# GELU MLP forward and backward on one core: the first block of x in two transposes from two queues, and a second copy moved ahead of a tanh

## The chip, the core and the metric

The kernel runs on one core of a Trainium2 chip. The metric is device time in microseconds, the median of several executions. One execution per kernel is also recorded by the hardware profiler; its trace gives the start and length of each instruction on TensorE (PE for matmuls, PEld for weight loads), VectorE (DVE), ScalarE (ACT) and GpSimd (POOL), and of each DMA issue on the queues of SyncE (SP), ScalarE and GpSimd. Times within the trace are us from the start of the profiled span.

## The reference

An MLP of one layer with the tanh form of GELU, forward and all gradients, in bf16. x is 2048 x 448, w1 448 x 1792, w2 1792 x 448.

```python
def _fwd_reference(x, w1, b1, w2, b2):
    h = jnp.einsum("bsd,df->bsf", x, w1) + b1
    h = _gelu(h)
    return jnp.einsum("bsf,fd->bsd", h, w2) + b2
...
    _out, _vjp = jax.vjp(_f, x, w1, b1, w2, b2)
    _grads = _vjp(grad_out)
    return (_out0, *[jnp.asarray(_g) for _g in _grads])
```

The outputs are the forward result, and the gradients of x, w1, b1, w2 and b2.

## The kernel before

**Tiling.** The 2048 rows are cut into four blocks of 512 (SB), taken in the order 512, 1024, 1536, 0 (ROW0). The 1792 hidden columns are 14 tiles of 128, taken as seven pairs per block in the order FP = 1, 2, ..., 6, 0. A step is one pair of one block, 28 steps in all. The 448 model columns are three full tiles of 128 and a tail of 64.

**A step.** For a pair, PE makes u = x w1 transposed (hidden columns on the partitions, 512 rows along the free dimension): six matmuls of 512 columns over the full tiles (`pe_u_fulls`, L207) and, for each half of the pair, a tail matmul of 64 partitions (`u_tail`, L222), which needs the tail rows of w1 (`wt1`) and closes the accumulation. `copy_u` brings u with its bias to SBUF: on ACT (L262) or DVE (L264). ACT makes its square (L271), its gelu (hT, L268) and, once DVE has made the cubic Z from the square (`dve_cubic`, L275 and L276), a tanh of it (`act_tanh`, L280). DVE turns these into the factor of the derivative (`dve_gate`, L284 to L291). PE makes q, the gradient with respect to h, from grad_out and w2 transposed (`q_tail` L229, `pe_q_fulls` L253), and DVE multiplies both into ghT (`dve_gh`, L294). The matmuls of the output and of the gradient of x follow in pieces (L323).

**Phases.** After the steps come the gradients of w1 (L562, L573) and w2 (L594) with x, grad_out, h and the h gradient in natural layout, while DVE sums the bias gradients.

**Order.** The kernel is written under a manual schedule: every engine runs its instructions in the order in which they are written, and the framework puts the waits between the engines. Queue order is also the order written. No wait is written out by hand.

**The start.** `zero` is cleared by DVE (L134). x's first block is brought in transposed, as xT (128 partitions, 4 column tiles, 512 rows), by one DMA transpose issued on SP's queue (`load_x`, L103). ScalarE's queue loads w1's columns 256 to 512 in two DMAs, the full tiles (L120) and the tail rows (L121); then it runs a gelu on one column, which brings in the activation table (L142), and loads the columns 512 to 768 in two further DMAs. SP's queue goes on with w1's columns 768 to 1024, two tiles of w2, the first block of grad_out transposed (`load_g`, gT, L113), the first part of w2 transposed (`load_w2T`, w2T, L128) and the rest in turn. All transposes of the kernel stand on SP's queue. PE runs 15 matmuls on `zero` (L168), nine of 512 columns and six of 256, before the first u.

After that PE makes u of step 0, and the order of the first steps is written out: copy of u(0) on ACT and DVE, square, gelu, cubic, u(1), tanh(0), the copies of u(1) on ACT, its square and gelu, u(2) and so on; from step 1 on a loop has a fixed order.

Of the kernel before, what the change touches and what calls it, by code (L numbers as in the profile page):

```python
# [11 lines left out]
BF16 = mybir.dt.bfloat16  # L12
# [7 lines left out]
def kernel(  # L20
# [15 lines left out]
    nc = tc.nc  # L36
    P = 128
    B, S, D = x.shape
# [4 lines left out]
    KF = D // P  # L43
    DL = D - KF * P
    SB = 512
# [3 lines left out]
    NSTEP = NB * NPAIR  # L49
    NSINGLE = 8  # L50
    LEAD = 2
    STG = 5
    ROW0 = [SB, 2 * SB, 3 * SB, 0]
    WIDE = (0, 1)
# [3 lines left out]
    x2 = x.rearrange("b s d -> (b s) d")  # L58
# [4 lines left out]
    const = ctx.enter_context(tc.tile_pool(name="const", bufs=1))  # L63
    dram = ctx.enter_context(tc.tile_pool(name="dram", bufs=1, space=bass.MemoryType.DRAM))
    psum = ctx.enter_context(tc.tile_pool(name="psum", bufs=1, space=bass.MemoryType.PSUM))
    blk = ctx.enter_context(tc.tile_pool(name="blk", bufs=2))
    tmp = ctx.enter_context(tc.tile_pool(name="tmp", bufs=2))
    stg = ctx.enter_context(tc.tile_pool(name="stg", bufs=STG))

    hT_dram = dram.tile([F, S], BF16, name="hT_dram")  # L70
    hT_dram_v = hT_dram.rearrange("(ft p) s -> p ft s", p=P)

    zero = const.tile([P, SB], BF16, name="zero")
    b1_rows = const.tile([32, P], BF16, name="b1_rows")
    b1_t16 = const.tile([P, 32], BF16, name="b1_t16")
    b1T = const.tile([P, NF], F32, name="b1T")
# [2 lines left out]
    w1_f = const.tile([P, KF, F], BF16, name="w1_f")  # L79
    w2T = const.tile([P, KF + 1, F], BF16, name="w2T")  # L80
    wt1 = const.tile([P, F], BF16, name="wt1")
# [6 lines left out]
    def one_bank(n, name):  # L88
        return psum.tile([P, SB], F32, name=name, tag=f"one{n}")

    def two_banks(n, name):
        return psum.tile([P, 2, SB], F32, name=name, tag=f"two{n}")

    xT, gT = {}, {}

    def wide(src, r0, n, shift):
        return bass.AP(src.tensor, src.offset + r0 * D - shift, [[D, n], [1, (KF + 1) * P]])

    def load_x(b):
        t = blk.tile([P, KF + 1, SB], BF16, name="xT", tag="xT")  # L100
        r0 = ROW0[b]
        if b in WIDE:
            nc.sync.dma_start_transpose(out=t[:], in_=wide(x2, r0, SB, 0))  # L103
        else:
            nc.sync.dma_start_transpose(out=t[:, 0:KF, :], in_=x2[r0:r0 + SB, 0:KF * P])
            nc.sync.dma_start_transpose(out=t[:, KF, :], in_=x2[r0:r0 + SB, D - P:D])
        xT[b] = t

    def load_g(b):
# [6 lines left out]
            nc.sync.dma_start_transpose(out=t[:, 0, :], in_=g2[r0:r0 + SB, 0:P])  # L116
        gT[b] = t

    def load_w1(eng, f0, f1):
        eng.dma_start(out=w1_f[:, :, f0:f1], in_=w1[0:KF * P, f0:f1].rearrange("(kt p) f -> p kt f", p=P))  # L120
        eng.dma_start(out=wt1[0:DL, f0:f1], in_=w1[KF * P:D, f0:f1])  # L121

    def load_w2(eng, t0, t1):
        eng.dma_start(out=w2_sb[:, t0:t1, :], in_=w2[t0 * P:t1 * P, :].rearrange("(ft p) d -> p ft d", p=P))
# [11 lines left out]
    nc.vector.memset(row0[:], 0.0)  # L136
    nc.vector.memset(row0[0:1, :], 1.0)
    nc.gpsimd.dma_start(out=b1_rows[0:NF, :], in_=b1.rearrange("(ft p) -> ft p", p=P))
    load_x(0)
    load_w1(nc.scalar, 256, 512)  # L140
    warm = stg.tile([P, 1], F32, name="warm", tag="warm", bufs=1)
    nc.scalar.activation(out=warm[:], in_=zero[:, 0:1], func=ACT.Gelu_apprx_tanh)  # L142
    load_w1(nc.scalar, 512, 768)
    load_w1(nc.sync, 768, 1024)
    load_w2(nc.sync, 2, 4)
    load_g(0)
# [17 lines left out]
    load_g(1)  # L164

    pw = two_banks(1, "pw")
    for w in [SB] * 9 + [SB // 2] * 6:
        nc.tensor.matmul(pw[:, 0, 0:w], lhsT=zero[:, 0:P], rhs=zero[:, 0:w], start=True, stop=True)  # L168
    for c in range(P // 32):
        nc.vector.transpose(b1_t16[c * 32:(c + 1) * 32, :], b1_rows[:, c * 32:(c + 1) * 32])  # L170
    nc.vector.tensor_copy(out=b1T[:], in_=b1_t16[:, 0:NF])
# [2 lines left out]
    PU, PQ = {}, {}  # L174
# [5 lines left out]
    def cols(p, a):  # L180
        return slice((2 * FP[p] + a) * P, (2 * FP[p] + a + 1) * P)

    def part(store, ks):
        return store[ks[0] // 2 % len(store)][:, 2 * (ks[0] % 2):2 * (ks[-1] % 2) + 2, :]
# [14 lines left out]
    def pe_u_fulls(f):  # L199
        b, p = divmod(f, NPAIR)  # L200
        if p == 0:
            hT[b] = blk.tile([P, NF, SB], BF16, name="hT", tag="hT")
        banks = (2, 3) if f == 1 else (0, 1) if f < NSINGLE + LEAD else order_a[2 * (f % 2):2 * (f % 2) + 2]
        PU[f] = [one_bank(n, "pu") for n in banks]
        for a in range(2):
            for kt in range(KF):
                nc.tensor.matmul(PU[f][a][:], lhsT=w1_f[:, kt, cols(p, a)], rhs=xT[b][:, kt, :], start=(kt == 0), stop=False,  # L207
                                 skip_group_check=True)

    def half(up):  # L210
        return slice(DL, P) if up else slice(0, DL)
# [1 line left out]
    def open_q(k):  # L213
        b, p = divmod(k, NPAIR)
        if p == 0:
            ghT[b] = blk.tile([P, NF, SB], BF16, name="ghT", tag="ghT")
        PQ[k] = two_banks(0 if k < NSINGLE else order_b[k % 2], "pq")

    def u_tail(f, a):
        b, p = divmod(f, NPAIR)  # L220
        hf = half(b not in WIDE)
        nc.tensor.matmul(PU[f][a][:], lhsT=wt1[hf, cols(p, a)], rhs=xT[b][hf, KF, :], start=False, stop=True,  # L222
                         tile_position=(hf.start, 0), skip_group_check=True)

    def q_tail(k, a, swap=False):
        b, p = divmod(k, NPAIR)
        hf = half((b in WIDE) != swap)
        g = g_swap[b] if swap else gT[b][:, 0, :]
        nc.tensor.matmul(PQ[k][:, a, :], lhsT=w2T[hf, 0, cols(p, a)], rhs=g[hf, :], start=True, stop=False,  # L229
                         tile_position=(hf.start, 0), skip_group_check=True)  # L230

    def pe_tails(fs, ks):
        cross = bool(fs) and bool(ks) and (fs[0] // NPAIR in WIDE) != (ks[0] // NPAIR in WIDE)
        for k in ks:
            open_q(k)
        us = [(f, a) for f in fs for a in range(2)]
        qs = [(k, a) for k in ks for a in range(2)]
        if not us and len(ks) == 2:
            for a in range(2):
                q_tail(ks[0], a)  # L240
                q_tail(ks[1], a, swap=True)
            return
        for n in range(max(len(us), len(qs))):
            if n < len(us):
                u_tail(*us[n])
            if n < len(qs):
                q_tail(*qs[n], swap=cross)
# [8 lines left out]
    def copy_u(f, engines):  # L256
        p = f % NPAIR
        for a in range(2):
            bias = b1T[:, 2 * FP[p] + a:2 * FP[p] + a + 1]
            dst = part(U4, [f])[:, a, :]  # L260
            if engines[a] == "a":
                nc.scalar.activation(out=dst, in_=PU[f][a][:], func=ACT.Identity, bias=bias)  # L262
            else:
                nc.vector.tensor_scalar(out=dst, in0=PU[f][a][:], scalar1=bias, scalar2=None, op0=ALU.add)  # L264
# [5 lines left out]
    def act_square(ks):  # L270
        nc.scalar.activation(out=part(A4, ks), in_=part(U4, ks), func=ACT.Square, scale=math.sqrt(3.0 * GELU_A * GELU_C))  # L271
# [6 lines left out]
    def act_tanh(ks):  # L278
        z = part(Z4, ks)
        nc.scalar.activation(out=z, in_=z, func=ACT.Tanh, scale=-1.0 / 3.0)  # L280
# [103 lines left out]
    def traffic(i):  # L384
# [5 lines left out]
        if i == 6:  # L390
            other_halves()

    pe_u_fulls(0)
    pe_tails([0], [])
    copy_u(0, "av")
    act_square([0])
    act_gelu([0])
    dve_cubic([0])
    pe_u_fulls(1)
    pe_tails([1], [])  # L400
    act_tanh([0])
    copy_u(1, "aa")
    act_square([1])
    act_gelu([1])
    pe_u_fulls(2)
    pe_tails([2], [])
    open_two(1, 2)
# [13 lines left out]
    for i in range(1, NSINGLE):  # L421
        f = i + LEAD
        pe_u_fulls(f)
# [219 lines left out]
```

## Time and profile before

| What | us |
|---|---|
| median of 3 runs | 273.18 (273.09 to 273.20) |
| profiled execution, device time | 273.36 |
| profiled execution, span | 271.56 |
| PE busy | 265.9 (98%) |
| DVE busy | 175.9 (65%) |
| ACT busy | 139.6 (51%) |
| warm-up matmuls L168 | 1.18 to 6.19 |
| first matmul of u(0) (L207) / first tail (L222) | 6.03 / 7.42 |
| first copy of u(0) on ACT / on DVE | 7.84 / 8.06 |

The span is the time from the first to the last instruction of the kernel in the trace; device time also has what lies around it. The chain of waits is followed back from the last instruction, at each step to what released it. Matmuls are pipelined: a row "x6, 1.46" has six matmuls whose starts lie some 0.215 apart, and the last one's latency behind them. For DMAs, an issue has a start and a length on its queue, and a time from issue to landing, after which its data may be used.

### The profile page before, as it was taken

The numbers are of one execution on the slowest core, as the hardware profiler recorded it, in microseconds if no ns is written. First come the engines' busy times: TensorE is split into PE (matmuls) and PEld (weight loads), VectorE is DVE, ScalarE is ACT, GpSimd is POOL, SyncE is SP. The second block draws the span as 40 slices with busy tenths as digits, with TensorE's granted clock in tenths as the row PEclk, the third lists the DMA queues.
The fourth block names the chain that finished last, engine by engine and source line by source line (L and its number), as shares of the span: only waits on it lengthen the run. The fifth ranks groups of instructions, "written<-read, shape, count | busy, mean of one in ns | idle before, by whom it ended". The sixth has DMA issues, their size and how long they took to land.

```text
span 271.6 us, 3646 instructions
## 1 busy us (share of the span) xinstructions
PE 265.9 (98%) x1397; PEld 127.2 (47%) x1411; DVE 175.9 (65%) x208; ACT 139.6 (51%) x163; POOL 38.4 (14%) x50
## 2 busy tenths in 40 slices
PE   8999999999999999999999999999999999999995
PEld 3334344444444545444454455554444485555554
DVE  2688999999989799685979931109999992000000
ACT  2799898799995687867668610011111121111111
POOL 1000004011001001010010102210510007900000
PEclk9999999999999999999999999999999999999999
DMA  8999799999999967074252559998111111999951
GB/s 188 224 205 238 139 213 179 167 270 249 226 265 256 239 164 170 18 191 97 93 125 75 111 108 289 377 223 199 40 41 39 39 41 30 199 212 238 196 129 34
DMA packets 112929, 44.37 MB, mean 163 GB/s; under 512 B 92000, under 2 KB 111792, under 8 KB 112912
## 3 DMA queue, kind: packets, MB, share of 16 engines
q1 hardware_dynamic: 105840, 36.20, 62.3%
q0 software_dynamic: 1824, 4.27, 5.2%
q10 hardware_dynamic: 5248, 3.67, 4.5%
q8 instruction: 11, 0.18, 0.3%
q14 instruction: 6, 0.05, 0.1%
HBM read 7.23 MB, written 14.23 MB: 79 GB/s over the span
## 4 chain that ended last, share of the span: by engine, by line
PE 87%; DVE 6%; ACT 5%; issue 1%; DVEq 0%; ACTq 0%
PE ps L323 28%; PE ps_v L594 16%; PE ps_w L562 13%; PE pq L253 11%; PE pu L207 10%; PE pu L222 4%; PE ps_w L573 2%; PE pw L168 2%; ACT A L271 1%; DVE ghT L294 1%; ACT U L262 1%; ACT hT L268 1%; DVE Z L276 1%; PE pq L229 1%; DVE Z L291 1%; DVE A L286 1%
## 5 line engine op out<-in xcount | busy, mean ns | idle before, releaser
L323 PE MATMUL ps<-w_sb,hT 128*128 128x448 bf16 x224 | 45.2, 352 | 0.2
L323 PE MATMUL ps<-w1T_sb,ghT 128*128 128x448 bf16 x224 | 43.8, 352 | 0.0
L262 ACT ACTIVATE U<-pu,b1T 128x512 bf16<-128x512 f32 x55 | 33.8, 685 | 18.3 <-PE pu L222 18.2
L594 PE MATMUL ps_v<-g_nat,h_nat 128*128 128x448 bf16 (+1 forms) x240 | 42.6, 340 | 0.0
L337 POOL DMA_DIRECT2D out_dram<-st x32 | 17.8, 558 | 162.6 <-ACT st L334 107.6
L253 PE MATMUL pq<-gT,w2T 128*128 128x512 bf16 x163 | 38.8, 380 | 0.5 <-issue 0.3
L207 PE MATMUL pu<-xT,w_f 128*128 128x512 bf16 x159 | 38.7, 379 | 0.4
L294 DVE SCALAR_TENSOR_TENSOR ghT<-Z,pq 128x1024 bf16<-128x1024 bf16 x28 | 33.8, 1220 | 7.5 <-PE pq L253 6.0
L562 PE MATMUL ps_w<-gh_nat,x_nat 128*128 128x512 bf16 (+1 forms) x192 | 36.7, 352 | 0.0
L280 ACT ACTIVATE Z<-Z 128x2048 bf16<-128x2048 bf16 (+1 forms) x18 | 27.5, 1528 | 10.4 <-DVE Z L276 10.2
L594 PEld LDWEIGHTS <-h_nat 128*128 128x128 bf16 x240 | 23.3, 98 | 19.3 <-issue 0.3
L323 PEld LDWEIGHTS <-hT 128*128 128x128 bf16 x224 | 21.8, 98 | 21.7 <-issue 1.1
L323 PEld LDWEIGHTS <-ghT 128*128 128x128 bf16 x224 | 21.9, 98 | 20.9
L548 DVE TENSOR_TENSOR acc<-acc,gh_nat 128x1792 f32<-128x1792 f32 x14 | 30.0, 2142 | 0.5
L271 ACT ACTIVATE A<-U 128x1024 bf16<-128x1024 bf16 (+1 forms) x19 | 27.7, 1456 | 0.7 <-DVE U L264 0.4
L268 ACT ACTIVATE hT<-U 128x1024 bf16<-128x1024 bf16 (+1 forms) x20 | 27.7, 1390 | 0.2
L562 PEld LDWEIGHTS <-x_nat 128*128 128x128 bf16 x192 | 18.7, 98 | 17.8 <-issue 0.4
L253 PEld LDWEIGHTS <-w2T 128*128 128x128 bf16 x168 | 15.0, 98 | 23.2 <-issue 7.6
L597 ACT CAST st<-ps_v 128x448 bf16<-128x448 f32 (+1 forms) x15 | 7.6, 507 | 34.8 <-PE ps_v L594 32.3
L207 PEld LDWEIGHTS <-w_f 128*128 128x128 bf16 x168 | 16.3, 98 | 19.1 <-issue 0.8
L334 ACT CAST st<-ps 128x448 bf16<-128x448 f32 x20 | 10.3, 529 | 27.7 <-PE ps L323 27.5
L565 ACT CAST st<-ps_w 128x512 bf16<-128x512 f32 (+1 forms) x12 | 6.4, 532 | 29.9 <-PE ps_w L562 29.9
(46 smaller groups left out, 197.3 us busy)
## 6 DMA issues: line engine op xcount, KB each, us to landing
hT_dram<-hT SPq DMA_DIRECT2D x28, 256.0 KB, 3.3
out_dram<-st POOLq DMA_DIRECT2D x32, 112.0 KB, 3.1
x_nat<-in_x_dram SPq DMA_DIRECT2D x1, 1792.0 KB, 10.2
g_nat<-in_grad_out_dram SPq DMA_DIRECT2D x1, 1792.0 KB, 16.0
out_dram<-st ACTq DMA_DIRECT2D x13, 112.0 KB, 3.3
out_dram<-st ACTq DMA_DIRECT2D x9, 128.0 KB, 1.7
w_sb<-in_w_dram SPq DMA_DIRECT2D x5, 224.0 KB, 3.9
w_f<-in_w_dram SPq DMA_DIRECT2D x5, 192.0 KB, 4.9
```

The source lines that it names most:

```text
L207: nc.tensor.matmul(PU[f][a][:], lhsT=w1_f[:, kt, cols(p, a)], rhs=xT[b][:, kt, :], start=(kt == 0), stop=False, skip_group_check=True)
L253: nc.tensor.matmul(PQ[k][:, a, :], lhsT=w2T[:, kt, cols(p, a)], rhs=gT[b][:, kt, :], start=False, stop=(kt == KF), skip_group_check=True)
L262: nc.scalar.activation(out=dst, in_=PU[f][a][:], func=ACT.Identity, bias=bias)
L268: nc.scalar.activation(out=rows(hT, r), in_=part(U4, r), func=ACT.Gelu_apprx_tanh)
L271: nc.scalar.activation(out=part(A4, ks), in_=part(U4, ks), func=ACT.Square, scale=math.sqrt(3.0 * GELU_A * GELU_C))
L280: nc.scalar.activation(out=z, in_=z, func=ACT.Tanh, scale=-1.0 / 3.0)
L294: nc.vector.scalar_tensor_tensor(out=rows(ghT, [k]), in0=part(Z4, [k]), scalar=1.0, in1=PQ[k][:], op0=ALU.add, op1=ALU.mult)
L323: nc.tensor.matmul(self.ps, lhsT=src[self.b][:, 2 * p + a, self.j * P:(self.j + 1) * P], rhs=w[:, 2 * FP[p] + a, :], start=(p == 0 and a = ...
L337: nc.gpsimd.dma_start(out=(out2 if self.kind == "o" else gx2)[r:r + P, :], in_=st[:, 0:D])
L548: nc.vector.tensor_tensor(out=v, in0=in0, in1=gh_nat[:, b, :, j, :], op=ALU.add)
L562: nc.tensor.matmul(ps[:, 0:n * P], lhsT=x_nat[:, st_, kt * P:(kt + 1) * P], rhs=gh_nat[:, b, ft0:ft0 + n, j, :], start=(st_ == 0), stop=(s ...
L594: nc.tensor.matmul(ps[:, 0:w], lhsT=h_nat[ft][:, st_, :], rhs=g_nat[:, st_, h * w:(h + 1) * w], start=(st_ == 0), stop=(st_ == NS - 1))
```

## The change

Four edits:

- x's first block is loaded in two transposes of 256 rows each, the first issued on SP's queue, the second on ScalarE's queue, after the full tiles of w1's columns 256 to 512 and ahead of that range's tail rows. The other loads of ScalarE's queue (columns 512 to 768) go to SP's queue, right behind the first half of x.
- The first u is computed by row halves: for rows 0 to 255 both hidden tiles' full matmuls, then the same for rows 256 to 511; the tail matmuls stay whole.
- The warm-up is 32 matmuls of 128 columns, and `zero` has 128 columns instead of 512.
- The two copies of the second u on ACT are written ahead of the first tanh instead of behind it.

```diff
+    NWAKE = 32
...
-    zero = const.tile([P, SB], BF16, name="zero")
+    zero = const.tile([P, P], BF16, name="zero")
...
+    def load_w1_full(eng, f0, f1):
+        eng.dma_start(out=w1_f[:, :, f0:f1], in_=w1[0:KF * P, f0:f1].rearrange("(kt p) f -> p kt f", p=P))
+
+    def load_w1_rest(eng, f0, f1):
+        eng.dma_start(out=wt1[0:DL, f0:f1], in_=w1[KF * P:D, f0:f1])
+
     def load_w1(eng, f0, f1):
-        eng.dma_start(out=w1_f[:, :, f0:f1], in_=w1[0:KF * P, f0:f1].rearrange("(kt p) f -> p kt f", p=P))
-        eng.dma_start(out=wt1[0:DL, f0:f1], in_=w1[KF * P:D, f0:f1])
+        load_w1_full(eng, f0, f1)
+        load_w1_rest(eng, f0, f1)
...
-    load_x(0)
-    load_w1(nc.scalar, 256, 512)
+    xT[0] = blk.tile([P, KF + 1, SB], BF16, name="xT", tag="xT")
+    halves = [slice(0, SB // 2), slice(SB // 2, SB)]
+    nc.sync.dma_start_transpose(out=xT[0][:, :, halves[0]], in_=wide(x2, ROW0[0], SB // 2, 0))
+    load_w1_full(nc.scalar, 256, 512)
+    nc.scalar.dma_start_transpose(out=xT[0][:, :, halves[1]], in_=wide(x2, ROW0[0] + SB // 2, SB // 2, 0))
+    load_w1_rest(nc.scalar, 256, 512)
     warm = stg.tile([P, 1], F32, name="warm", tag="warm", bufs=1)
     nc.scalar.activation(out=warm[:], in_=zero[:, 0:1], func=ACT.Gelu_apprx_tanh)
-    load_w1(nc.scalar, 512, 768)
+    load_w1(nc.sync, 512, 768)
...
-    for w in [SB] * 9 + [SB // 2] * 6:
-        nc.tensor.matmul(pw[:, 0, 0:w], lhsT=zero[:, 0:P], rhs=zero[:, 0:w], start=True, stop=True)
+    for w in range(NWAKE):
+        nc.tensor.matmul(pw[:, 0, 0:P], lhsT=zero[:], rhs=zero[:], start=True, stop=True)
...
-        for a in range(2):
-            for kt in range(KF):
-                nc.tensor.matmul(PU[f][a][:], lhsT=w1_f[:, kt, cols(p, a)], rhs=xT[b][:, kt, :], start=(kt == 0), stop=False,
-                                 skip_group_check=True)
+        for rs in halves if f == 0 else [slice(0, SB)]:
+            for a in range(2):
+                for kt in range(KF):
+                    nc.tensor.matmul(PU[f][a][:, rs], lhsT=w1_f[:, kt, cols(p, a)], rhs=xT[b][:, kt, rs],
+                                     start=(kt == 0 and rs.start == 0), stop=False, skip_group_check=True)
...
+    copy_u(1, "aa")
     act_tanh([0])
-    copy_u(1, "aa")
```

## The prediction

> **What bounds the kernel now.** I read the page's busy times first, then the chain of waits in order of time, then the timeline of the first 42 us, then the DMA landings by issue.
>
> ```profile
> PE 265.9 (98%) x1397; PEld 127.2 (47%) x1411; DVE 175.9 (65%) x208; ACT 139.6 (51%) x163; POOL 38.4 (14%) x50
> ```
>
> TensorE (PE) is busy 265.9 of 271.6 us. The change touches only the first 14 us, so what counts is when PE's useful work starts and whether anything makes it stop before it runs on without a break.
>
> ```profile
> 1.18 5.01 PE pw L168 x15
> 6.19 1.29 PE pu L207 x6
> 7.49 0.55 PE pu L222 x2
> ...
> 8.06 0.76 DVE U L264
> ...
> 8.91 1.06 ACT A L271
> ...
> 11.19 1.06 ACT Z L280
> 12.24 1.16 ACT U L262 x2
> ...
> 22.64 0.44 DVE Z L275
> ...
> 36.83 1.23 DVE ghT L294
> ...
> 38.11 0.37 PE pq L229
> ```
>
> The columns are start, length and work. The chain goes from the warm-up matmuls (L168) to the first u (L207, then its tail L222), over ScalarE (ACT) until 22.6, over VectorE (DVE) until 38.06, and from there on PE to the end. The start of the first tail, at 7.42 in the timeline, is thus the head of everything.
>
> ```profile
> 0.72 1.42 SPq L103 DMA_TRANSPOSE xT<-in_x_dram  x1
> ...
> 1.23 0.55 ACTq L121 DMA_DIRECT2D wt<-in_w_dram  x1
> ...
> 4.75 2.97 SPq L113 DMA_TRANSPOSE gT<-in_grad_out_dram  x1
> ...
> 7.76 1.30 SPq L128 DMA_TRANSPOSE w2T<-in_w_dram  x1
> ...
> 11.19 1.06 ACT L280 ACTIVATE Z<-Z 128x1024 bf16<-128x1024 bf16 x1 [0.27 <-DVE Z L276]
> ```
>
> These are the issues that the change moves, and the one ACT idle (0.27) that its last part removes.
>
> ```profile
> 22.02 1.46 PE L207 MATMUL pu<-xT,w_f 128*128 128x512 bf16 x6
> ...
> 26.76 1.46 PE L207 MATMUL pu<-xT,w_f 128*128 128x512 bf16 x6
> ...
> 37.66 0.39 PE L222 MATMUL pu<-xT,wt 64*128 64x512 bf16 x1
> ...
> 38.12 0.39 PE L222 MATMUL pu<-xT,wt 64*128 64x512 bf16 x1
> ```
>
> PE's steps come 4.74 us apart from 22.02 and wait for nothing until the two tails at 37.66 and 38.12. In the steps before, such a pair starts 0.23 apart (18.66, 18.89), so PE stops there for 0.46-0.23 = 0.23 us: it waits for DVE's ghT, which ends at 38.06. PE and the ACT/DVE chain are 0.23 us apart; a delay of the first tail moves both, and a gain on ACT alone is worth 0.23 at most.
>
> ```profile
> xT<-in_x_dram SPq DMA_TRANSPOSE x1, 5.1
> ...
> wt<-in_w_dram ACTq DMA_DIRECT2D x1, 32.0 KB, 3.9
> ...
> w2T<-in_w_dram SPq DMA_TRANSPOSE x1, 3.6
> ```
>
> The last column is us from issue to landing: x's 512 rows land at 0.72+5.1 = 5.82, the weights' tail rows (wt1, 256:512) at 1.23+3.9 = 5.13. The w2T row is a transpose of 256 rows by 512 columns, the very size of half of x.
>
> **The halves of x.** The first half is issued at 0.72 on SyncE's queue (SP). Its landing isn't in the trace: 3.6 by the w2T row (4.3 in the second of that size, issued at 10.79), 5.1 at most by the whole block. x's packets went at 969 in the us from 3 to 4, so the half's 1024 fewer packets are worth 1.06 us: 5.1-1.06 = 4.0. I take 3.9: it lands at 4.6.
>
> The second half is issued by ScalarE behind one w1 issue (0.72 to 1.18). No transpose in this trace comes from ScalarE, so no row shows whether it runs beside the first or waits for it. Both bounds: it starts at 1.23, or it waits for the landing at 4.6 and starts at 4.65. No wait is written in the kernel; the framework places them. I read it as keeping transposes of two queues apart, and take the wait; it is an assumption, and the other case is the first rival. The Trainium skill, DMA: Bandwidth & Descriptors, section "Silent corruption: two transposing streams in flight at once", asks for just this wait: the later stream's first transpose has to wait for the full completion of the earlier one, SP and ACT being two streams. No run here shows it; by it the sum is the one below, without it the first rival's.
>
> With the wait, ScalarE issues from 4.65 to 5.95 (1.30 as L128) and the half lands 3.6 later, at 8.25 (bounds 3.5, the w2T transpose of 240 rows issued at 29.84, and 4.3: 8.15 to 8.95). Behind the waiting instruction on ScalarE's queue stands the load of wt1 256:512, which the first tail needs. It is issued at 6.0 instead of 1.23. The seven loads of 32 KB landed in 3.7 to 5.0; the queues are emptier here, so I take 3.7: 9.7. The lower bound is the 2.8 of w1's first load: 8.8. The table load and the warm activation (1.28+0.20) also stand behind; they end by 8.1, before ACT's first copy.
>
> **The first u.** PE does the first half's six 256-column matmuls from 4.6 and the second half's from 8.25. Together they are as many columns as before: 6 x 0.215 = 1.29 us, so 0.65 for the second half, ending at 8.9, with six more weight loads of 98 ns under them. The tail then waits for wt1 until 9.7. It starts 9.7-7.42 = **+2.3 us** later. Bounds: 3.5 in place of 3.9 for the first half and 2.8 for wt1 give a tail at 8.42, +1.0; 4.3 and 5.0 give 11.4, +4.0.
>
> **Warm-up.** Zero shrinks to the size of the row0 memset beside it (0.11 for 0.27), so PE starts at 1.02. A 512-column warm-up matmul took 0.43 (weight loads at 2.01, 2.44, 2.87), so 128 columns are 0.107 if columns set the pace, 0.18 if it is the pace of the 256-column ones (five loads in 0.91). The 32 end at 4.4 to 6.8, before 8.25 either way: 0 on the path.
>
> **What SP does meanwhile.** It has two more issues (w1 512:768 and its tail rows, 0.5 each), and x's is shorter. w1 512:768 starts at about 2.1 instead of 1.87 and lands by 7.2 (5.1); the second u needs it at 7.96+2.3 = 10.3: 0. The next transpose on SP, gT, waits in turn for ScalarE's half: 8.3 instead of 4.75, so SP and all queued behind it is 3.55 late. w2T 256:512 lands at 7.76+3.6+3.55 = 14.9; PE wants it at 13.92+2.3 = 16.2. x's second block lands at 26.60+5.8+3.55 = 35.95; PE wants it at 36.27+2.1 = 38.4. So every load stays covered, with 1.3 us to spare at the tightest of these two; a tail that comes only 1.0 late would leave 0.0 and put the rest, us for us, on PE.
>
> **Second u copied ahead of tanh.** u(1) is complete at 9.95 and ACT's gelu ends at 10.91; the two copies (1.16) fill the idle of 0.27 and go on while DVE finishes Z. Everything behind on ACT is 0.27 earlier. What waits for tanh is DVE's Z+1 at 12.66, 0.5 us later; it is hidden by DVE's idle of 0.71 before 14.52. The end gains what PE stops for: **-0.2**.
>
> **Sum.** +2.3-0.2 = +2.1 on the profiled execution: 273.36 (span 271.56 and 1.8 around it), so 275.46. That execution is 0.18 above the median of 273.18; against the median it is **275.3**. Own range, by +1.0 and +4.0: 274.0 to 277.0.
>
> **The rivals.**
>
> *No wait between the halves: faster.* ScalarE issues its half from 1.23 to 2.53 and wt1 from 2.6, which lands at 6.5. Both halves are in by 5.82, since the same bytes went over the same engines. PE ends the fulls by 6.5, the tail starts at 6.6 in place of 7.42: -0.8-0.2 = -1.0, **272.2**. For it: the code names two queues and no wait. Against: the reading above. It decides as soon as the first tail starts before 7.6; past that the change can't gain.
>
> *The wait, and PE at half speed again: 276.7.* In the warm-up a 512-column matmul took 0.43, from 6.19 on 0.215: PE is at full speed only after some 4.8 us of work. The profile's PEclk row says 9 from the first slice, against these spacings. Now PE works from 1.02 to about 5.9, just 4.8, stops until 8.25 and works little until 9.7. If it is slow at 9.7 and stays so until 4.8 us after 8.25, it does 3.35 us at half speed and loses 1.7; less the 0.23 by which PE is ahead of DVE that is +1.5 to the 275.3, so about 276.7. The Trainium skill, TensorE: Matmul & The Clock Gate, section "What's actually happening", has half rate as the state at rest, released by a busy window of some 3.4 us and taken back by an idle one. The slow first matmuls agree with that; by it gaps of 2.35 and 0.8 us alone would not bring half rate back, and this rival needs a warm-up that never got through.
>
> *The wait, but short: 274.0.* Half and wt1 at their fastest (tail +1.0) and w2T on time. For it: the queues are emptier. Against: no 32 KB load landed in under 3.7.
>
> **How the numbers follow.** Wait and full speed 0.45, wait and half speed 0.33, short wait 0.10, no wait 0.12. The likeliest gives 275.3. From 273.9 to 277.2 holds the short wait, the forecast with most of its bounds and the half speed without its worst: a little over 8 in 10; the no-wait case lies outside. A measurement here tells about 0.2% (0.55 us) from no change: faster 0.10, the no-wait case with little lost; same 0.05, what is left of that and of the short wait; slower 0.85.
>
> **What would show it.** In the profile after: the transpose on ScalarE's queue starts at about 4.65 (1.23 if the rival holds); wt1 256:512 is issued right behind it; gT on SP starts after 8; the first L222 starts near 9.7; gaps in PE between 5.9 and 9.7; the first matmuls after that 0.215 apart (0.43 if slow); the two copies of the second u end ahead of the first tanh, with no ACT idle between gelu and them; PE's steps 4.74 apart later on. A ScalarE transpose that is issued before the first has landed would make the prediction wrong, and so would a first tail before 8.4.

## The result and the profile after

The changed kernel takes 277.40 us (median of 6 runs, 276.29 to 278.11) beside 273.19 for the kernel before on the same chip (6 runs): a ratio of 1.0153, 95% interval 1.0129 to 1.0176. It is 4.2 us slower; 2.1 were forecast, and the value lies 0.2 above the range. The profiled execution took 277.47 with a span of 275.7, 4.1 above the span before.

The page of the changed kernel: busy times, then from its table of 40 slices (6.9 us each) the rows of PE and of the granted clock.

```profile
PE 268.2 (97%) x1434; PEld 129.4 (47%) x1434; DVE 175.7 (64%) x208; ACT 139.8 (51%) x163; POOL 38.2 (14%) x50
...
PE   6799999999999999999999999999999999999995
...
PEclk9599999999999999999999999999999999999999
```

PE is busy 2.3 us more, and the second slice of the clock row says 5 for the 9 of all the others: half speed for much of the time between 6.9 and 13.8. The loss is all at the start. The chain of waits of the changed kernel, in order of time:

```profile
0.73 3.80 DMA xT<-in_x_dram
4.55 4.21 DMA xT<-in_x_dram
8.80 1.44 PE pu L219 x6
10.24 0.96 PE pu L234 x2
11.21 2.67 PE pu L219 x6
13.88 0.97 PE pu L234 x2
14.85 1.40 PE pu L219 x6
16.25 0.54 PE pu L234 x2
16.78 1.62 PE ps L335 x8
```

It begins with the two halves of x, one behind the other, and from 8.80 on it is PE almost to the end (L219 is the old L207, L234 the old L222, L335 the old L323). The timeline of the same stretch has the queues:

```profile
2.13 0.56 SPq L121 DMA_DIRECT2D w_f<-in_w_dram  x1
...
4.55 1.34 ACTq L150 DMA_TRANSPOSE xT<-in_x_dram  x1
4.57 0.81 PE L219 MATMUL pu<-xT,w_f 128*128 128x256 bf16 x6
...
5.93 0.60 ACTq L124 DMA_DIRECT2D wt<-in_w_dram  x1
...
8.80 1.44 PE L219 MATMUL pu<-xT,w_f 128*128 128x256 bf16 x6 [3.42 <-DMA xT<-in_x_dram]
...
8.84 1.91 SPq L114 DMA_TRANSPOSE gT<-in_grad_out_dram  x1
10.17 0.13 PEld L234 LDWEIGHTS <-wt 64*128 64x128 bf16 x2 [0.41 <-issue]
```

The first half lands at 0.73+3.8 = 4.53, and ScalarE's transpose is issued at 4.55. That half lands at 4.55+4.2 = 8.76, and gT, which stood ready on SP's queue after 5.11, is issued at 8.84. PE idles 3.42 us between the halves. By the rule of the Trainium skill, DMA: Bandwidth & Descriptors, section "Silent corruption: two transposing streams in flight at once", a transpose on another queue has to wait for the full completion of the one before: the issue times in this trace are those of such a wait, twice over.

The same execution by stages: busy time of PE, PEld, DVE, ACT and POOL, then the granted clock, the DMA share and GB/s.

```profile
4.57:5.40 0.83, 0.81 (x7) 0.58 (x6) 0.76 (x5) 0.00 (x0) 0.00 (x0) 1.00 0.80 230
5.40:8.80 3.40, 0.00 (x0) 0.00 (x0) 0.12 (x1) 1.49 (x2) 0.00 (x0) 0.88 0.84 179
8.80:14.80 6.00, 6.00 (x17) 1.74 (x17) 2.23 (x5) 3.04 (x4) 0.00 (x0) 0.50 0.82 178
14.80:18.30 3.50, 3.50 (x17) 1.29 (x16) 2.63 (x6) 3.50 (x5) 0.00 (x0) 1.00 1.04 225
```

The clock was up when the first half of u ran (six matmuls of 256 columns in 0.81). It fell during the idle stretch (0.88 is a mean; narrower stretches of the same view put the fall at 7.95, 2.6 us after PE had stopped) and was 0.50 for the whole of the next 6.0 us of work. So the account of this execution, step by step against the kernel before: the first tail starts at 10.17 for 7.42, **+2.75**, of which 0.7 is the second half's matmuls at half speed (8.80 to 10.17, 1.37 for 0.65). From there to the third u (14.78 for 9.89 in the timelines) PE takes 4.61 for 2.47, **+2.14**. The first q comes only 4.41 later (18.33 for 13.92), since the eight output matmuls before it (L335) no longer stop, **-0.48**. PE's stop near 38 is gone, **-0.22** (the eighth u starts 4.40 later, 40.67 for 36.27, the ninth 4.19, 46.40 for 42.21). The sum is 4.19, and the last group of matmuls starts 4.18 later; the spans differ by 4.11.

### The profile page after: what moved, and what is told of

It reads as the page before. It is cut to its first block, busy times and chain, and to the rows that moved or that the text cites. A ratio compares the mean times of both kernels' runs of the same rounds, so it can differ in the third digit from the quotient of the medians.

```text
span 275.7 us, 3707 instructions
## 1 busy us (share of the span) xinstructions
PE 268.2 (97%) x1434; PEld 129.4 (47%) x1434; DVE 175.7 (64%) x208; ACT 139.8 (51%) x163; POOL 38.2 (14%) x50
## 4 chain that ended last, share of the span: by engine, by line
PE 96%; DMA 3%; ACT 0%; issue 0%
PE ps L335 31%; PE ps_v L606 15%; PE pq L265 14%; PE pu L219 14%; PE ps_w L574 13%; PE pu L234 5%; DMA xT<-in_x_dram 3%; PE ps_w L585 2%; PE pq L241 1%; PE ps L339 0%; ACT st L609 0%
## 5 line engine op out<-in xcount | busy, mean ns | idle before, releaser
L335 PE MATMUL ps<-w_sb,hT 128*128 128x448 bf16 x224 | 44.8, 352 | 0.0
L219 PE MATMUL pu<-xT,w_f 128*128 128x512 bf16 (+1 forms) x174 | 41.5, 385 | 3.4 <-DMA xT<-in_x_dram 3.4
L335 PE MATMUL ps<-w1T_sb,ghT 128*128 128x448 bf16 x224 | 43.8, 352 | 0.0
L265 PE MATMUL pq<-gT,w2T 128*128 128x512 bf16 x168 | 39.4, 380 | 0.0
L335 PEld LDWEIGHTS <-hT 128*128 128x128 bf16 x224 | 21.8, 98 | 21.2 <-ACT Z L292 0.4
L335 PEld LDWEIGHTS <-ghT 128*128 128x128 bf16 x224 | 21.9, 98 | 20.9
L219 PEld LDWEIGHTS <-w_f 128*128 128x128 bf16 x174 | 17.4, 101 | 24.1 <-issue 6.5
```

The lines of the kernel that those rows point to most:

```text
L219: nc.tensor.matmul(PU[f][a][:, rs], lhsT=w1_f[:, kt, cols(p, a)], rhs=xT[b][:, kt, rs], start=(kt == 0 and rs.start == 0), stop=False, ski ...
L265: nc.tensor.matmul(PQ[k][:, a, :], lhsT=w2T[:, kt, cols(p, a)], rhs=gT[b][:, kt, :], start=False, stop=(kt == KF), skip_group_check=True)
L335: nc.tensor.matmul(self.ps, lhsT=src[self.b][:, 2 * p + a, self.j * P:(self.j + 1) * P], rhs=w[:, 2 * FP[p] + a, :], start=(p == 0 and a = ...
```

## The experiments

Each was timed beside the kernel before on the same chip, whose median lay between 273.29 and 273.56. Ratios are against it, with 95% intervals. A ratio need not be the quotient of the two medians beside it, least of all where the executions fall into two groups (short warm-up alone: 1.0048 by the medians).

| Run | median us | before | ratio, 95% interval |
|---|---|---|---|
| one queue | 272.62 | 273.52 | 0.9972 (0.9955 to 0.9988) |
| copy alone | 272.67 | 273.52 | 0.9973 (0.9964 to 0.9981) |
| two queues alone | 276.61 | 273.52 | 1.0109 (1.0084 to 1.0135) |
| filler | 275.41 | 273.52 | 1.0072 (1.0056 to 1.0087) |
| two pieces | 273.81 | 273.29 | 1.0013 (1.0004 to 1.0021) |
| short warm-up alone | 274.60 | 273.29 | 1.0019 (1.0001 to 1.0038) |
| one queue, w1 back | 274.45 | 273.29 | 1.0037 (1.0026 to 1.0047) |
| both on ScalarE | 277.71 | 273.29 | 1.0157 (1.0138 to 1.0176) |
| one queue, w1's last part on ScalarE | 275.20 | 273.56 | 1.0074 (1.0052 to 1.0096) |
| tail rows first | 276.49 | 273.56 | 1.0117 (1.0099 to 1.0136) |
| one queue, long warm-up | 273.32 | 273.56 | 1.0007 (0.9983 to 1.0031) |

**One queue.** The theory after the result: the wait between two queues, and the clock that PE loses in it. Rivals: the halves and the load order cost by themselves, or the short warm-up does. One word of the changed kernel is changed:

```diff
-    nc.scalar.dma_start_transpose(out=xT[0][:, :, halves[1]], in_=wide(x2, ROW0[0] + SB // 2, SB // 2, 0))
+    nc.sync.dma_start_transpose(out=xT[0][:, :, halves[1]], in_=wide(x2, ROW0[0] + SB // 2, SB // 2, 0))
```

> The changed kernel with the second half of x issued on SyncE's queue too, right behind the first; all else as changed. Theory (the wait between the transposes of two queues, and the clock lost in it, are the whole cost): no wait, second half lands by 6.0, first tail at 6.6 to 7.2, gT issued at about 5, no half clock after 6; 272.1 to 273.2. Rival A (halves, more matmuls and the other load order cost by themselves): the time stays above 275.5. Rival B (the short warm-up alone costs, as the clock is not released in time): 274 to 275.5 with 512-column matmuls 0.43 apart in the second u.

Measured: 0.9972, as the theory had it; the 4.2 us are gone. Its timeline:

```profile
2.13 1.28 SPq L150 DMA_TRANSPOSE xT<-in_x_dram  x1
...
5.32 1.47 PE L219 MATMUL pu<-xT,w_f 128*128 128x256 bf16 x12 [0.75 <-DMA xT<-in_x_dram]
...
6.49 2.58 SPq L114 DMA_TRANSPOSE gT<-in_grad_out_dram  x1
6.72 0.11 PEld L234 LDWEIGHTS <-wt 64*128 64x128 bf16 x2 [0.21 <-issue]
```

On one queue the second transpose is issued as soon as the first is (2.13), and the twelve matmuls of 256 columns run through at full speed; the tail starts at 6.72, 3.45 earlier than in the changed kernel. gT is late by its place behind two more issues, not by a wait. So the halves as such cost nothing that shows here: the twelve matmuls take 1.47 in all, as the six of 512 columns did (1.46).

**Two queues alone.** The other side of the same test: the kernel before, with x in two transposes from two queues and nothing else changed.

```diff
-    load_x(0)
-    load_w1(nc.scalar, 256, 512)
...
+    nc.sync.dma_start_transpose(out=xT[0][:, :, halves[0]], in_=wide(x2, ROW0[0], SB // 2, 0))
+    nc.scalar.dma_start(out=w1_f[:, :, 256:512], in_=w1[0:KF * P, 256:512].rearrange("(kt p) f -> p kt f", p=P))
+    nc.scalar.dma_start_transpose(out=xT[0][:, :, halves[1]], in_=wide(x2, ROW0[0] + SB // 2, SB // 2, 0))
+    nc.scalar.dma_start(out=wt1[0:DL, 256:512], in_=w1[KF * P:D, 256:512])
```

> The kernel before with only x's first block in two transposes, the second on ScalarE's queue between the full tiles and the tail rows of w1's columns 256 to 512; long warm-up, whole first u and tanh order as before. Theory: the second half lands at 8.8, PE stops from 6.2 to 8.8, first tail at 10.1 if the clock stays up (275.5 to 276.0), 11.5 if it drops (277.0 to 279.0); in no case under 275. Rival A (the short warm-up and the halves of u are what costs): 273.2 to 273.8.

Measured: 1.0109, +3.1 us. From its timeline:

```profile
4.58 1.34 ACTq L143 DMA_TRANSPOSE xT<-in_x_dram  x1
...
8.07 2.71 PE L211 MATMUL pu<-xT,w_f 128*128 128x512 bf16 x6 [2.40 <-DMA xT<-in_x_dram]
```

And one of its stages, in the columns of the stages above:

```profile
8.80:12.00 3.20, 3.20 (x9) 0.79 (x8) 0.26 (x1) 0.64 (x1) 0.00 (x0) 0.57 0.91 190
```

The wait is there with the long warm-up and the whole first u as well, and after 2.4 us of idle PE the clock is down again: it fell at 8.12, when PE had just begun again. The time lies below the 277.0 to 279.0 that were expected with the clock down, as the second half landed earlier (7.94) and half speed lasted half as long as in the changed kernel (8.12 to 11.53). The short warm-up is not needed for the loss.

**Filler.** The clock's share by itself: the changed kernel with matmuls on zeros between the two halves.

```diff
         for rs in halves if f == 0 else [slice(0, SB)]:
+            if rs.start > 0:
+                for _ in range(56):
+                    nc.tensor.matmul(pw[:, 0, 0:P], lhsT=zero[:], rhs=zero[:], start=True, stop=True)
```

> The changed kernel with 56 further warm-up matmuls of 128 columns between the two halves of the first u, so that PE works while it waits for the second half; wait and landings as changed. Theory (the clock costs some 2.4 of the 4.2 us, the late tail the rest): granted clock 1.00 after 8.8, the second half 0.65 and the second u 1.3 long, first tail at 9.4 to 9.7; 274.6 to 275.2. Rival (the clock costs nothing at the end, the tail's lateness and SP's late loads are all): 277.0 to 277.8.

Measured: 1.0072, +1.9 for the +4.2 of the changed kernel, with the same wait (the second half is issued at 4.62, gT at 9.30 for 8.84). In its timeline the matmuls after the wait are quick:

```profile
9.26 0.82 PE L222 MATMUL pu<-xT,w_f 128*128 128x256 bf16 x6
...
10.01 0.11 PEld L237 LDWEIGHTS <-wt 64*128 64x128 bf16 x2 [0.21 <-issue]
```

The tail is 0.16 earlier than in the changed kernel, so what is saved is the work behind it: the clock costs some 2.3 us, and the wait without it the other 1.9, which are 2.6 of a late tail (10.01 for 7.42) less the 0.7 that follow.

**Copy alone.** The kernel before with the last part of the change only.

```diff
+    copy_u(1, "aa")
     act_tanh([0])
-    copy_u(1, "aa")
```

> The kernel before with only the copies of the second u written ahead of the first tanh. Theory: ACT's idle of 0.27 goes, PE's stop of 0.23 near 38 goes: 272.9 to 273.0, 0.2 less than before. Rival (the later tanh holds up DVE's gate and with it ghT): 273.2 or up to 273.7.

Measured: 0.9973, 0.7 us less, more than three times the forecast. The weight loads of the kernel before, from its timeline:

```profile
11.82 0.68 PEld L323 LDWEIGHTS <-hT 128*128 128x128 bf16 x5 [0.42 <-issue]
12.87 0.28 PEld L323 LDWEIGHTS <-hT 128*128 128x128 bf16 x2 [0.37 <-issue]
13.45 0.10 PEld L323 LDWEIGHTS <-hT 128*128 128x128 bf16 x1 [0.29 <-issue]
```

The same loads with the copies first:

```profile
11.88 1.25 PEld L323 LDWEIGHTS <-hT 128*128 128x128 bf16 x8 [0.42 <-ACT U L262]
13.50 0.11 PEld L229 LDWEIGHTS <-w2T 64*128 64x128 bf16 x2 [0.37 <-issue]
```

In the kernel before the eight loads of the first output pieces come in three groups. ACT's two copies of the second u end at 12.84 (12.15+0.69) and 13.40: the second and third group start 0.03 to 0.05 behind them. The third and fourth piece go into the banks of PSUM, PE's accumulators (`one_bank(2)`, `one_bank(3)`), that hold the second u until it is copied. With the copies first, the eight run without a stop and the first q starts at 13.51 for 13.92. The profile gave these stops the label "issue". PE's lead is not the whole of it: the chain of the kernel before runs over ACT and DVE until 38, so that had to come earlier too. It did, by more than the idle of 0.27: the second square starts at 12.96 for 13.43, and the ghT that PE waits for near 38 ends at 37.56 for 38.05, 0.49 earlier. PE's fourth u is 0.41 earlier (16.86 for 17.27) and the ninth 0.49 (41.72 for 42.21); the two profiled spans differ by 0.5. The two gains come with the same edit, and no run parts them.

**Two pieces.** A test of that reading: in the kernel before, only the two pieces in other banks go ahead of the first q. (The fourth u, at 17.27, is called the third in the text below.)

```diff
-    pieces(4, 0, -1)
+    pieces(2, 0, -1)
...
-    pieces(4, 1, -1)
+    pieces(6, 1, -1)
```

> The kernel before (tanh first, one transpose) with only two of the four first output pieces ahead of the first q; the other two, whose banks still hold the second u until ACT has copied it, go with the next pieces. Theory (PE's weight loads at 12.87 and 13.45 wait for these copies): no stop between the pieces, the third u starts 0.4 to 0.5 earlier (16.8 for 17.27), but the ACT and DVE chain up to 38 is not earlier, so the end stays: -0.3 to +0.1 against the kernel before. Rival (the copies' place among ACT's work alone made the gain, PE's stop there has another cause): the third u still starts near 17.3.

Measured: 1.0013, 0.1 to 0.6 slower. The stop between the pieces is gone (four matmuls in 0.93 from 12.39), but PE stops 0.79 at 16.05, where the pieces that moved wait for the second gelu, and the fourth u starts at 18.33 for 17.27. The first tail of this execution was also 0.57 late. It agrees with the reading of the banks and says nothing on what it is worth.

**Tail rows first.** The prediction had w1's tail rows land last. Here they are issued ahead of ScalarE's transpose.

```diff
+    load_w1_rest(nc.scalar, 256, 512)
     nc.scalar.dma_start_transpose(out=xT[0][:, :, halves[1]], in_=wide(x2, ROW0[0] + SB // 2, SB // 2, 0))
-    load_w1_rest(nc.scalar, 256, 512)
```

> The changed kernel with the tail rows of w1's columns 256 to 512 issued on ScalarE ahead of the second half of x instead of behind it. Prediction's step (the tail rows land last and set the first tail): first tail 0.8 or more earlier, 276.6 or less. What the trace of the changed kernel shows instead (they landed at 8.93, the second half's matmuls ran until 10.2): first tail unchanged within 0.2 of the end of these matmuls, 276.9 to 278.1.

Measured: 276.49, inside what the prediction's step gave, but the trace has another reason: the tail rows landed at 1.23+3.7 = 4.9, and the first tail still started at 10.30, right behind the second half's matmuls (8.94 to 10.30), 0.13 later than in the changed kernel. So the tail rows do not set the first tail. What differs is the clock: full speed was back before the second u was done, which took 1.94 (11.27 to 13.21) for 2.67. As the executions of the changed kernel alone spread over 1.8 us, the time says little here and the trace decides.

**Short warm-up alone.** The kernel before with 32 matmuls of 128 columns and the smaller `zero`.

```diff
-    for w in [SB] * 9 + [SB // 2] * 6:
-        nc.tensor.matmul(pw[:, 0, 0:w], lhsT=zero[:, 0:P], rhs=zero[:, 0:w], start=True, stop=True)
+    for w in range(32):
+        nc.tensor.matmul(pw[:, 0, 0:P], lhsT=zero[:], rhs=zero[:], start=True, stop=True)
```

> The kernel before with only the short warm-up (32 matmuls of 128 columns, smaller zero); x in one transpose. PE idles from 4.6 to 6.0. Theory (a stop of 1.4 us does not drop the clock, since a window of 3.4 with work in it stays up): 273.2 to 273.8, matmuls of the first u 0.215 apart. Rival (the short warm-up by itself fails to bring the clock up): matmuls of the first and second u 0.43 apart, 274.5 to 276.5.

Measured: neither alone. Four of ten executions took 273.0 to 273.2, as the theory had it, six 274.6 to 275.8, as the rival had it; the ratio is 1.0019. The profiled one (275.84) is of the second kind: the first u's weight loads are 0.43 apart from 6.75 on, and half speed ends only at the second tail (12.55). Its clock row says 1.00 all the while, so at the start of a trace the spacing is the safer reading. 3.6 us of warm-up bring the clock up in some executions and not in others.

**Both on ScalarE.** To see whether it is the change of queue that costs, the first half goes to ScalarE too.

```diff
-    nc.sync.dma_start_transpose(out=xT[0][:, :, halves[0]], in_=wide(x2, ROW0[0], SB // 2, 0))
+    nc.scalar.dma_start_transpose(out=xT[0][:, :, halves[0]], in_=wide(x2, ROW0[0], SB // 2, 0))
```

> The changed kernel with the first half of x on ScalarE's queue too, so that both halves come from ScalarE and only gT on SyncE's queue has to wait for another queue's transpose. Theory (the cost is the alternation of two queues, not ScalarE's queue): second half issued without a wait by 4, lands by 6.5, first tail at 7.0 to 8.0; gT waits until the half has landed, which is at most 0.5 later than it could be issued; 0.3 to 1.3 less than the kernel before. Rival (transposes from ScalarE's queue are slow, or gT's wait costs): first tail after 8.5, 274.5 or more.

Measured: 1.0157, not what the theory had. The second half is issued without a wait, at 2.75, but lands after 6.1, at 8.89; w1's full tiles, between the two transposes, take 5.3 and land at 7.4, where PE starts, after 2.84 of idle and at half speed (the twelve matmuls take 2.95 for 1.47). gT waits until 8.98. ScalarE's queue is not slow by itself: the same half took 4.2 from it in the changed kernel and 3.4 in two queues alone. SP meanwhile loads five pieces of w1 and w2 that the first u doesn't need; that these take the transfers' share is likely and wasn't tried by itself. So this run leaves the alternation of queues as it was shown by the first two, and adds that leaving it out is not enough.

**Towards a better kernel.** In the one-queue run PE waits at 44.7 for w1's transpose (w1T_sb), 0.8 at its weight load, and the start gained in front is lost there: its span is 0.2 below that of copy alone (270.8 and 271.0), for a first tail 0.76 earlier. Three attempts to keep it. The first, against the one-queue run:

```diff
-    load_w1(nc.sync, 512, 768)
+    load_w1(nc.scalar, 512, 768)
```

> Both halves of x on SyncE's queue as in the run with one queue, and w1's columns 512 to 768 back on ScalarE's queue. Theory (in that run the earlier start was lost at 44.7, where PE waited for w1's transpose, issued 0.8 later behind the two moved loads): w1's transpose lands by 43.9, no wait there, and the first tail 0.75 earlier reaches the end: 1.2 to 1.6 less than the kernel before. Rival (the loss at 44.7 has another cause): 0.6 to 0.9 less, as with one queue.

Measured: 1.0037, worse. With these loads beside it the first half of x lands at 5.97 instead of 5.3, PE idles 1.44 behind the short warm-up, and the clock isn't up: the twelve matmuls of the first u take 2.72 for 1.47. The question of 44.7 wasn't reached.

The second, against the one-queue run:

```diff
-    NWAKE = 32
+    NWAKE = 44
```

> Both halves of x on SyncE's queue and 44 warm-up matmuls instead of 32, so that PE works until the first half has landed. Theory (the late executions of the one-queue run and of the short warm-up are those in which the clock was not up when the warm-up ended): all executions within 0.5 of each other, 0.6 to 0.9 less than the kernel before. Rival (the spread has another cause): again a tenth or more of the executions 1.4 above the others.

Measured: 1.0007, nothing gained, and the executions spread from 272.5 to 276.6: the rival holds. In the profiled one PE does not stop ahead of the first u and the first tail is at 7.08, but an issue on SP at 14.72 takes 2.51 for some 0.5, and the weight loads wait 1.4 for w1 and 1.6 for w1's transpose. What held up that issue, and whether the other late executions lost their time in the same place, no trace shows.

The third, against the second:

```diff
-    load_w1(nc.sync, 0, 256)
...
     act_square([1])
+    load_w1(nc.scalar, 0, 256)
     act_gelu([1])
```

> Both halves of x on SyncE's queue, copies ahead of tanh, 44 warm-up matmuls, and w1's columns 0 to 256 issued by ScalarE between the second square and the second gelu instead of on SyncE's queue. Theory (with one queue the start is 0.75 earlier, and lost at 44.7 to w1's transpose that SyncE issues too late): w1's transpose is issued about 1.1 earlier, no wait for it, 1.1 to 1.5 less than the kernel before. Rival (the two issues on ScalarE hold up its chain, or the transpose is not earlier): 0.3 to 0.9 less, as with one queue or worse.

Measured: 1.0074. w1's transpose is issued 0.6 earlier than with one queue (33.37 for 33.98) and PE does not wait for it, but ScalarE's own work stands behind the two issues: its second gelu starts at 16.00 instead of some 13.6 (an idle of 2.3). The issues take 0.48 and 0.50 and start at 14.33 and 15.45; what holds them so long isn't shown. The copy alone and the one-queue run come out best and equal within their intervals, 0.7 below the kernel before, and below the changed kernel by 4.9; the copy alone is the smaller edit and spreads less (272.5 to 273.2, one queue 272.1 to 274.0).

## Why the prediction was right and wrong

**The direction and the wait were right.** ScalarE's transpose waits for SP's (4.55 for the 4.65 forecast), gT for ScalarE's (8.84 for 8.3), the first tail is late (10.17 for 9.7), PE idles between the halves, every later load stayed covered. The rival without a wait (272.2) fell; it describes the one-queue kernel (272.62), which is the change without its second queue.

**The step that failed: full speed behind the wait.** Of the two cases with the wait, "wait and full speed" was taken at 0.45 and gave the sum; "PE at half speed again" had 0.33. It was half speed, and its loss was put too low: 3.35 us at half speed, 1.7 lost, from work up to 4.8 us after 8.25. In the profiled execution PE ran at 0.50 from 8.80 to 14.80 and lost 0.7 ahead of the tail and 2.14 behind it; by the filler run the clock costs 2.3 of the 4.2. What that run leaves, 1.9, is near the 2.1 of the sum by luck: a tail 2.6 late for 2.3 and an order of copies worth 0.7 for 0.2. With the case right and the size as forecast (276.7) the value would have been 0.7 short. The argument for the case was also wrong in one point: the warm-up did get through (first half of u at full speed, clock 1.00 up to 5.40); it was the idle stretch that took the clock back. The Trainium skill, TensorE: Matmul & The Clock Gate, section "What's actually happening", has an idle window of some 3.4 us take it back. The traces differ from that: PE stood still for 3.42 here, but the clock fell 2.6 us into it, and in the run with two queues alone PE stood still for only 2.40 and the clock fell too. So the reason for which the prediction took this case to need a warm-up that never got through does not hold: 3.4 us without work were not needed.

**What ends last before the first tail was wrong.** The step "the tail then waits for wt1 until 9.7" put wt1's landing at 3.7 after its issue; it took 3.0 (8.93). The second half took 4.2 for 3.6, and its matmuls 1.37 for 0.65; the tail started behind them, and with the tail rows loaded first it still did (10.30). That the tail is only 0.47 off is luck, two errors of opposite sign.

**The copy was mis-sized.** "The end gains what PE stops for: -0.2" took ACT's chain as 0.27 earlier and PE as free to gain only its stop near 38. The three groups of weight loads at 11.82, 12.87 and 13.45 stood in the trace, their label "issue" named no releaser, and the banks shared with the second u were not looked at: in the changed kernel, where the chain is PE's from 8.80 on, that is 0.48 more. Alone the copies are worth 0.7, with PE and the chain over ACT and DVE each some 0.5 earlier in the trace.

**Halves, warm-up.** The halves cost nothing, as forecast (one queue). The warm-up was put at "0 on the path": that holds behind the long wait, but the short one fails to bring the clock up in some executions when nothing follows it at once.

## What to carry to other kernels

A transpose by DMA that goes to another queue than the one before is not a second lane: it started only when the other had landed, and the next transpose of the first queue waited in turn; ask of every load moved between queues what it must now wait for. Price a stop of PE of some 2.4 us or more by the work behind it at half speed, not by its own length: here the clock cost 2.3 of 4.2 us. And where a trace calls a stop "issue", look for the buffer that ends at the same moment; moving two copies ahead of a tanh gained 0.7 by itself, as much as the best form of the whole change (one queue).

## What was not expected of the hardware

- The clock fell 2.6 us after PE had stopped in the changed kernel and after 2.4 us of idle PE in two queues alone. It stayed at half for 6.8 us in the first (7.95 to 14.78) and for 3.4 in the second (8.12 to 11.53) and with the tail rows first (8.98 to 12.39). In the two short cases PE worked through these 3.4 us almost from their start; in the long one it stood still for the first 0.85. Whether that decides between 3.4 and 6.8 was not tried by itself. After a warm-up of 3.6 us and 1.8 us of idle PE was at half speed in the profiled execution; by their times it was not in four of ten.
- A half of x took from 3.4 to 6.1 us to land. That this goes by what else was loading is likely and wasn't tried by itself: 3.8 first on its queue with the other half held back, 5.2 with the other half and w1's next columns right beside it.
- ScalarE's DMA issues held its compute: two issues between a square and a gelu left ACT idle for 2.3 us, of which the issues themselves are 0.98.
